# A fused attention and gated feed-forward block: who gets which of two accumulator banks

## The chip, the core and the metric

One NeuronCore of a Trainium2 chip runs the whole kernel. The time is that of one execution on the device, in microseconds (us), and the number compared is the median over several executions. The engines in the profile: PE is TensorE (PEld its weight loads), DVE VectorE, ACT ScalarE, POOL GpSimd, and SP issues most DMAs. TensorE writes only into PSUM, eight banks of 512 fp32 columns by 128 partitions; ACT and DVE read it out.

## The reference

`x` has 2048 tokens of width 512; 32 heads of width 16 attend to a window of 256 tokens; the feed-forward part has 1792 hidden columns.

```python
x = A_x
xn = _layernorm(x, axis=-1)
s = _A_ref(xn, A_wqkv, A_wo)               # causal window attention, W = 256, then @ wo
g = _silu(_B_ref(xn, B_w1, B_w3, B_w2))    # (silu(xn @ w1) * (xn @ w3)) @ w2
return x + s * g
```

## The kernel before

The tokens are cut into four tiles `t` of 512, the heads into four groups `g` of eight, the hidden columns into 14 blocks `f` of 128. Every fp32 operand is split into a high and a low f16 half, and a product is three f16 products (high by high, low by high, high by low) added up in one bank. A dense product of one 128 x 512 result is thus twelve matmuls of 512 columns, issued as two pieces of six: queries and keys (`project`, L442), values (`value`, L412), gate and up (`gate_up`, L712), down (`down`, L757), output (`total`, L799).

PSUM has three pools. `pss` (two tiles of two banks) holds the scores, `pso` (two banks) the attention's result. `psm` has the two banks that matter here; all dense products use them, and so do three short users: the transposes of an input block (`turn`, L374), the little column sums behind a weight's scale (`powers`, L222), and the transpose of the scores' maxima (`finish` in `pass1`, L511). Before, all of these ask for a tile of one tag with two buffers (`tag="mm"`), and the tile layer assigns the buffer.

Who reads a bank: a gate product is read by ACT (tanh, L723) and one step later by DVE (L727); an up product by DVE (L732); a projection by ACT (L451) and then DVE (L455); a value product by ACT (L415); a down product by DVE (L773), or ACT (L770) the first time; a turned block by ACT (L377) and then DVE (L382); maxima by ACT (L514); column sums by DVE (L224).

TensorE's order is the order in which the program issues (`ORDERED`); the other engines' order is set by a scheduler with priorities (`urgent` raises one). The attention goes by 32 units (a tile, a group, half of its heads). In each unit `batches` makes small batches of score matmuls, `pass1` for the unit after next (scores, row maxima on DVE, L500) and `pass2` for this one (scores again, L547; mask, L554; exponentials, L557; times values, L573), and `spread` lays the pieces of dense products between them. After each batch and each piece with matmuls, `step` counts `now` up by one and runs what `later(n, f)` put off by `n` steps.

In the first tile (t = 0) the feed-forward weights arrive as fp32 (`load`, L647 and L649), are squared and summed for a scale (`measure`, `squares`, L197 and L199), and split (`split_pool`: ACT scales in place, L246, ACT makes the high half, L247, POOL the low one, L243). The halves go to DRAM (L717, L760) and are loaded from there for the other tiles. All of these tiles live in 32 slots of SBUF of one size: `take` takes the slot that has been free longest, `give` puts one back, and the tile layer makes the new owner wait for the last reader of the old one. SP issues the DMAs in order, so a load that waits for its slot holds back those behind it.

```python
    def take(dtype):
        slot = free.pop(0)
...
    def give(*tiles):
        for made in tiles:
            free.append(held.pop(id(made))[0])
```

Of the kernel before, what the change touches and what calls it, by code (L numbers as in the profile page):

```python
# [76 lines left out]
def tile_block(ctx: ExitStack, tc: tile.TileContext, x, wqkv, wo, w1, w3, w2, out):  # L77
# [18 lines left out]
    psm = pool("psm", 2, PSUM)  # L96
# [4 lines left out]
    free = [f"slot{i}" for i in range(SLOTS)]  # L101
    held = {}

    def take(dtype):
# [5 lines left out]
    def give(*tiles):  # L110
        for made in tiles:
            free.append(held.pop(id(made))[0])
# [11 lines left out]
    now = [0]  # L124
# [20 lines left out]

    def flush():
        while queue:
            step()

# [30 lines left out]

    V = const.tile([P, VB, H * VW + DH], F32, name="V")
# [7 lines left out]
    def squares(parts, on_act=0, apart=0):  # L189


        ssq = small.tile([P, len(parts)], F32, name="ssq")

        def one(i, raw):
            sq = ppool.tile([P, D], BF16, name="sqa" if i < on_act else "sqd", bufs=2)
# [12 lines left out]
        def cast():  # L208
            nc.vector.tensor_copy(sb, ssq)
        if apart:  # L210
            later(apart * (len(parts) + 1) // 2, cast)
        else:
            cast()
        return sb

    def powers(sb, n, p2, inv):


        ps = psm.tile([P, n], F32, name="ps", tag="mm") if started else pss.tile([P, 2, 512], F32, name="s")[:, 0, 0:n]
        m = sb.shape[-1] // n  # L220
        for i in range(m):
            nc.tensor.matmul(ps, onesb, sb[:, i * n:(i + 1) * n], start=i == 0, stop=i == m - 1)  # L222
        al = small.tile([P, n], F32, name="al")
        nc.vector.tensor_scalar(al, ps, 2.08, 1e-30, op0=ALU.mult, op1=ALU.max)  # L224
# [103 lines left out]
    def prepare(t):  # L328
# [32 lines left out]
        def turn(b):  # L361
            if t not in X:
                X[t] = xpool.tile([P, NC, TW], F16, name="XH"), xpool.tile([P, NC, TW], F16, name="XL")
            xh, xl = X[t]
            c = slice(b * P, (b + 1) * P)

            if t or b == 3:
                pt = psm.tile([P, NC, P], F32, name="mm", tag="mm")
            elif b == 2:
                pt = pso.tile([P, 2, TW], F32, name="po")[:, 0, :].rearrange("p (k q) -> p k q", q=P)  # L370
            else:
                pt = pss.tile([P, 2, 512], F32, name="s")[:, 0, :].rearrange("p (k q) -> p k q", q=P)
            for k in range(NC):
                nc.tensor.transpose(pt[:, k, :], xts[b][:, k * P:(k + 1) * P], identf)  # L374
            give(xts.pop(b))
            with urgent():
                lasts["xh"] = nc.scalar.copy(xh[:, :, c], pt)  # L377

            def rest():
                turned[t] = turned.get(t, 0) + 1  # L380
                with urgent():
                    lasts["x"] = nc.vector.tensor_sub(xl[:, :, c], pt, xh[:, :, c])  # L382
            later(1, rest)
        return load, stats, rstd, centre, turn

    def prepare_beside(t):
# [9 lines left out]
        return made, [(0, lambda b=b: later(1 + 2 * b, lambda: turn(b))) for b in range(4)]  # L396

    def value(j):
# [4 lines left out]
        def part(half):  # L403
# [3 lines left out]
            if half == 0:  # L407
                cell["pv"] = psm.tile([P, D], F32, name="mm", tag="mm")
# [17 lines left out]
    def project(t, g, k, terms=(range(3),)):  # L426
# [7 lines left out]
        def part(n):  # L434
# [3 lines left out]
            if n == 0:  # L438
                cell["pp"] = psm.tile([P, TW], F32, name="mm", tag="mm")
# [13 lines left out]
            def rest():  # L453
# [9 lines left out]
                give(both)  # L463
# [16 lines left out]
    def pass1(t, g, p):  # L480
# [3 lines left out]
        nm = small.tile([P, 2, 16], F16, name="nm")  # L484
# [23 lines left out]
        def finish():  # L508
            qa = QA[t, g]
            pm = psm.tile([32, P], F16, name="pm", tag="mm")  # L510
            nc.tensor.transpose(pm, nm.rearrange("p b i -> p (b i)"), identh)  # L511
            mt = small.tile([32, P], F16, name="mt")
            with urgent():
                nc.scalar.copy(mt, pm)  # L514
# [138 lines left out]
    def measure(f, apart=0):  # L653
# [4 lines left out]
        def scale():  # L658
# [10 lines left out]
            def cut(i):  # L669
                a = [take(F16) for _ in range(2)]  # L670
                WF[0, f + i] = [a, None]
                for k in range(2):
                    split_pool(a[k][:, 0:D], a[k][:, D:], raws[i][k], pi[:, k, i:i + 1])
                give(*raws[i])
            later(1, lambda: cut(0))
            later(2, lambda: cut(1))
        later(5 if apart else 4, scale)

    def measure_down(k):
# [10 lines left out]
        def cut(f):  # L690
            raw2 = RAW.pop(f)[1]
            WF[0, f][1] = b = take(F16)
            split_pool(b[:, 0:D], b[:, D:], raw2, sw[:, f - f0:f - f0 + 1])
            give(raw2)
# [6 lines left out]
    def gate_up(t, f):  # L701
        cell = {}

        def part(k, half):
# [3 lines left out]
            if half == 0:  # L708
                cell[k] = psm.tile([P, TW], F32, name="mm", tag="mm")
# [8 lines left out]
            give(w)  # L718
# [10 lines left out]
            else:  # L729
# [5 lines left out]
                def rest():  # L735
                    nc.scalar.copy(hh[:, 0:TW], sg)  # L736
                    halves(nc.gpsimd.tensor_sub, hh[:, TW:], sg, hh[:, 0:TW])
                    give(sg)
# [6 lines left out]
    def down(t, k, b):  # L745
# [4 lines left out]
        def part(fs):  # L750
            if fs[0] == f0:
                cell["ps"] = psm.tile([P, D], F32, name="mm", tag="mm")
# [27 lines left out]
    def total(t, b):  # L780
# [4 lines left out]
        def part(half):  # L785
            WOH, WOL = SQ["wo"][:2]
            tb = slice(b * P, (b + 1) * P)
            if half == 0:
                cell["ps"] = psm.tile([P, D], F32, name="mm", tag="mm")
# [11 lines left out]
            if half:  # L801
# [7 lines left out]
                give(y, XR[t, b])  # L809
        return opening([(6, lambda h=h: part(h)) for h in range(2)])  # L810

    def total_by_columns(t, b):
# [9 lines left out]
        for c in (slice(0, 256), slice(256, 512)):  # L822
            ps = psm.tile([P, 256], F32, name="mm", tag="mm")
# [70 lines left out]
    def batches(u, ahead):  # L894
# [10 lines left out]
        for k, pair in enumerate(pairs):  # L905
            take_cols = not ahead or (k and k % 2 == 0 if u else k == 1)

            def batch(pair=pair, end=k == len(pairs) - 1, take_cols=take_cols):
# [7 lines left out]
                if end and cols1:  # L916
                    late.append(cols1)
                for c in ready:
                    c()
            made.append((COLS * 2 * take_cols if u else 0, batch))  # L920
        return made

    def spread(made, dense):
# [4 lines left out]
        for k, (cost, batch) in enumerate(made):  # L928
# [3 lines left out]
            while dense and (at + dense[0][0] / 2 <= whole * (k + 1) / len(made) or dense[0][0] == 0):  # L932
                c, piece = dense.pop(0)
                at += c
                piece()
                if c:
# [3 lines left out]
    def run(dense):  # L940
        for c, piece in dense:
            piece()
            if c:
# [32 lines left out]
    def keep_busy(n):  # L976
        ps = psm.tile([P, 4, P], F32, name="ps", tag="mm")
# [28 lines left out]
    k00, q00 = (project(0, 0, k, ((0,), (1,), (2,))) for k in (1, 0))  # L1006
# [19 lines left out]
    run(project(0, 1, 0))  # L1026
    later(1, lambda: fetch(0, 1))
    measure(2, 1)
    run(value(0))
# [8 lines left out]
    later(3, qk[3][2])  # L1038
    later(5, qk[3][3])
# [23 lines left out]
    for n, u in enumerate(units):  # L1063
# [7 lines left out]
        if n == 7:  # L1071
            wout[1](2)
            later(12, wout[2])
            later(14, lambda: wout[3](2))
            later(15, out_scale)
# [9 lines left out]
    while late:  # L1085
# [4 lines left out]
        step()  # L1090
    for b in range(2):
# [33 lines left out]
```

## Time and profile before

| | |
|---|---|
| median of 3 runs | 892.08 us (892.05 to 895.04) |
| the profiled execution | 886.62 us |
| its span, first to last instruction | 884.4 us |
| mean granted clock of TensorE | 0.992 |
| moved by DMA | 110.56 MB |

A row of a group gives line, engine, operation, names, shapes and count, then busy time and mean duration of one (ns), then the engine's idle time before these instructions and what ended it. A row of the order of time gives start, duration, engine, line and names, and in brackets the idle time before with its releaser. Matmuls overlap, so their mean duration is longer than the time from one to the next.

### The profile page before, as it was taken

How to read it: one execution, taken by the hardware profiler on the slowest of the kernel's cores; microseconds unless marked ns; L12 is line 12 of the kernel's file. 1: busy time of each engine (PE TensorE's matmuls, PEld its weight loads, DVE VectorE, ACT ScalarE, POOL GpSimd, SP SyncE). 2: the span in 40 equal slices, each digit the busy share in tenths (PEclk: the TensorE clock that was granted, in tenths of full speed). 3: DMA queues.
4: the chain of work that ended last, by engine and by line, in shares of the span. 5: the costliest groups of instructions: out<-in, count | busy, mean ns of one | idle time of the engine just before them, and what ended most of it. 6: DMA issues, size and time to landing. Idle time of an engine off the chain costs nothing.

```text
span 884.4 us, 21601 instructions
## 1 busy us (share of the span) xinstructions
PE 839.2 (95%) x8327; PEld 370.2 (42%) x8327; DVE 602.3 (68%) x1961; ACT 415.4 (47%) x618; POOL 196.4 (22%) x314
## 2 busy tenths in 40 slices
PE   7898868999999999999999999999999999999997
PEld 3344324444444444444444444444444444444443
DVE  7787665777667657786767766676666777666335
ACT  6886666473434444334344344443444434443521
POOL 2255254242111202111120112120211103131211
PEclk9999999999999999999999999999999999999999
DMA  9974444636633434444334433534452353332301
GB/s 290 240 257 148 151 130 120 197 92 208 157 107 90 113 103 120 126 136 106 108 114 114 115 99 84 157 113 101 119 134 70 100 153 104 100 109 69 80 9 60
DMA packets 95318, 110.56 MB, mean 125 GB/s; under 512 B 17200, under 2 KB 60528, under 8 KB 95216
## 3 DMA queue, kind: packets, MB, share of 16 engines
q1 hardware_dynamic: 94928, 108.67, 43.5%
q8 instruction: 65, 1.06, 0.5%
q10 hardware_dynamic: 288, 0.52, 0.2%
q14 instruction: 37, 0.30, 0.1%
HBM read 76.28 MB, written 28.57 MB: 119 GB/s over the span
## 4 chain that ended last, share of the span: by engine, by line
PE 66%; DVE 12%; ACT 7%; issue 6%; POOL 4%; DMA 4%; SPq 1%; POOLq 0%; ACTq 0%; DVEq 0%
PE mm L712 24%; PE mm L757 14%; PE po L573 7%; PE mm L442 6%; PE s L547 4%; POOL slot L243 4%; PE s L495 4%; PE mm L799 3%; PE mm L412 3%; DVE junk L500 3%; ACT pt L557 2%; DVE s L554 2%; DMA slot<-in_B_w_dram 1%; DVE slot L732 1%; DMA dr<-dd 1%
## 5 line engine op out<-in xcount | busy, mean ns | idle before, releaser
L712 PE MATMUL mm<-XH,slot 128*128 128x512 f16 x896 | 269.7, 383 | 8.6 <-DVE slot L455 4.0
L243 POOL TENSOR_TENSOR slot<-slot,slot 128x256 f16<-128x256 f32 (+1 forms) x220 | 147.4, 696 | 499.9 <-ACT slot L736 350.3
L557 ACT ACTIVATE pt<-s,es 128x1024 f32<-128x1024 f32 x152 | 168.9, 1114 | 181.3 <-DVE s L554 175.9
L500 DVE CUSTOM_DVE_ANT_0 junk<-s,MW 128x320 bf16<-128x320 f32 x448 | 217.8, 486 | 43.6 <-PE s L495 33.7
L712 PEld LDWEIGHTS <-slot 128*128 128x128 f16 x1344 | 123.4, 98 | 167.0 <-issue 29.0
L554 DVE TENSOR_TENSOR s<-s,MK 128x256 f32<-128x256 f32 (+2 forms) x280 | 121.1, 435 | 76.7 <-PE s L547 70.8
L712 PE MATMUL mm<-XL,slot 128*128 128x512 f16 x448 | 170.8, 381 | 0.0
L757 PE MATMUL mm<-slot,slot 128*128 128x512 f16 x672 | 157.6, 382 | 0.6 <-DVE XL L382 0.2
L757 PEld LDWEIGHTS <-slot 128*128 128x128 f16 x672 | 61.9, 98 | 80.8 <-issue 12.1
L573 PE MATMUL po<-pt,V 64*32 64x320 f32 (+4 forms) x2880 | 89.7, 347 | 0.0
L495 PE MATMUL s<-KA,qa 48*64 48x320 f16 (+2 forms) x1024 | 72.8, 299 | 12.2 <-DVE M L500 6.2
L547 PE MATMUL s<-qa,KA 50*64 50x320 f16 (+3 forms) x1472 | 62.5, 261 | 4.3 <-DVE M L500 3.3
L736 ACT CAST slot<-slot 128x512 f16<-128x512 f32 x56 | 34.5, 616 | 62.0 <-DVE slot L732 61.6
L723 ACT ACTIVATE slot<-mm,sgs 128x512 f32<-128x512 f32 x56 | 38.4, 685 | 47.1 <-PE mm L712 44.3
L547 PEld LDWEIGHTS <-KA 50*64 50x64 f16 x1472 | 31.4, 105 | 68.4 <-issue 34.4
L243 POOL TENSOR_TENSOR on<-on,rb 128x256 f32<-128x256 f32 x32 | 23.1, 744 | 163.0 <-DMA qa<-dm 98.3
L727 DVE SCALAR_TENSOR_TENSOR slot<-slot,mm 128x512 f32<-128x512 f32 x56 | 38.4, 686 | 28.9 <-ACT slot L723 28.9
L732 DVE SCALAR_TENSOR_TENSOR slot<-mm,slot 128x512 f32<-128x512 f32 x56 | 38.5, 688 | 25.9 <-PE mm L712 25.3
L573 PEld LDWEIGHTS po<-pt,V 64*32 64x32 f32 x2880 | 43.8, 106 | 28.0 <-issue 7.2
L773 DVE SCALAR_TENSOR_TENSOR slot<-mm,dsc,slot 128x512 f32<-128x512 f32 x48 | 35.9, 748 | 26.3 <-PE mm L757 26.1
L442 PE MATMUL mm<-XH,whi 128*128 128x512 f16 x128 | 47.3, 381 | 4.7 <-DVE slot L455 1.6
L495 PEld LDWEIGHTS <-qa 48*64 48x64 f16 x1024 | 29.9, 106 | 45.2 <-issue 23.9
(129 smaller groups left out, 829.8 us busy)
## 6 DMA issues: line engine op xcount, KB each, us to landing
slot<-dW SPq DMA_DIRECT2D x126, 256.0 KB
slot<-in_B_w_dram SPq DMA_DIRECT2D x42, 256.0 KB
dW<-slot SPq DMA_DIRECT2D x42, 256.0 KB
slot<-in_A_x_dram SPq DMA_DIRECT2D x30, 256.0 KB
KA<-dK SPq DMA_DIRECT2D x24, 288.0 KB
qa<-dQ SPq DMA_DIRECT2D x32, 192.0 KB
dK<-slot SPq DMA_DIRECT2D x16, 256.0 KB
dQ<-slot SPq DMA_DIRECT2D x16, 256.0 KB
```

Source lines behind the costliest of these rows:

```text
L243: op(out[:, c], a[:, c], b[:, c])
L442: nc.tensor.matmul(cell["pp"], a[:, k, c, :], b[:, c, :], start=(c, i) == parts[0][0], stop=(c, i) == parts[-1][-1])
L495: nc.tensor.matmul(s[64 * c:64 * c + 64, r, :n], qa[rows, 2 * p + a, ii * P + 64 * c:ii * P + 64 * c + 64], ka[rows, 2 * p + a, e - n:e], ...
L500: nc.vector.tensor_tensor_reduce(out=junk[:, :n], in0=s[:, r, :n], in1=mask, scale=1.0, scalar=NEG, op0=ALU.add, op1=ALU.max, accum_out=M[ ...
L547: nc.tensor.matmul(s[64 * h:64 * h + 64, r, o:o + 64 * n], ka[rows, 2 * p + a, 64 * (m + 4):64 * (m + 5)], qa[rows, 2 * p + a, 64 * (m + k ...
L554: nc.vector.tensor_add(v, v, MK[:, kind, of:of + n, :].unsqueeze(1).to_broadcast([P, 2 * len(which), n, 64]))
L557: nc.scalar.activation(pt, s, AF.Exp, scale=es)
L573: nc.tensor.matmul(cell["po"][32 * i:32 * i + 32, h, 64 * (m + k):64 * (m + k + n)], V[64 * h:64 * h + 64, (4 * t + m // 2) % VB, hd * VW: ...
L712: nc.tensor.matmul(cell[k], w[:, (a * NC + c) * P:(a * NC + c + 1) * P], b[:, c, :], start=c == 0 and i == 0, stop=c == NC - 1 and i == 2)
L723: nc.scalar.activation(sg, cell[0], AF.Tanh, scale=sg_scale[:, f:f + 1])
L732: nc.vector.scalar_tensor_tensor(sg, cell[1], 0.5 * HS / (WS * XS)**2, sg, op0=ALU.mult, op1=ALU.mult)
L757: nc.tensor.matmul(ps, hh[:, a * TW + b * P:a * TW + (b + 1) * P], w[:, c * D:(c + 1) * D], start=f == f0 and i == 0, stop=f == f1 - 1 and ...
```

## The change

- `psm` gets one buffer for each of two tags, m0 and m1. `bank` gives a dense product the bank that the last dense product didn't have; a short user takes that other bank too, without moving the turn on.
- `later_in_bank` and `pump` put work off that uses a bank for a short time: it runs at the first piece, not before its due step, that leaves a product open. The scales of weights, the maxima's transposes and the turning of blocks go there. The maxima are transposed three steps after the last batch that made them; before, two batches into the next unit.
- The maxima stand in 32 columns of a 128 x 128 tile of zeros (three such tiles), and the whole tile is transposed.
- In the start-up, projections of group 0 (keys), group 1 (queries) and the first value product use score banks, and the turned blocks change places (two in `psm`, one each in `pso` and `pss`).
- `give` may say that a tile will still be read for some steps; `take` takes the slot whose reading ends first by that count.
- The four splits of a pair of blocks come one by one, 1, 2, 4 and 6 steps after their scale.

```diff
-    psm = pool("psm", 2, PSUM)
+    psm = pool("psm", 1, PSUM)
...
     def take(dtype):
-        slot = free.pop(0)
+        free.sort()
+        slot = free.pop(0)[2]
...
+    def give(*tiles, after=0):
         for made in tiles:
-            free.append(held.pop(id(made))[0])
+            given[0] += 1
+            free.append((now[0] + after, given[0], held.pop(id(made))[0]))
...
+    def later_in_bank(n, f):
+        made_so_far[0] += 1
+        banked.append((now[0] + n, made_so_far[0], f))
+
+    def pump():
+        due = min((q for q in banked if q[0] <= now[0]), default=None)
+        if due is not None:
+            banked.remove(due)
+            due[2]()
...
+    def bank(shape, dtype=F32, short=False):
+        b = 1 - open_bank[0]
+        if not short:
+            open_bank[0] = b
+        return psm.tile(shape, dtype, name=f"m{b}", tag=f"m{b}", bufs=1)
...
+    NM = [const.tile([P, P], F16, name=f"NM{i}") for i in range(3)]
+    for nm in NM:
+        nc.gpsimd.memset(nm, 0.0)
...
-            if t or b == 3:
-                pt = psm.tile([P, NC, P], F32, name="mm", tag="mm")
+            if t:
+                pt = bank([P, NC, P], short=True)
+            elif b < 2:
+                pt = bank([P, NC, P])
...
-        return made, [(0, lambda b=b: later(1 + 2 * b, lambda: turn(b))) for b in range(4)]
+        return made, [(0, lambda b=b: later_in_bank(1 + 2 * b, lambda: turn(b))) for b in range(4)]
...
-                cell["pp"] = psm.tile([P, TW], F32, name="mm", tag="mm")
+                cell["pp"] = pss.tile([P, 2, TW], F32, name="s")[:, 0, :] if scores_bank else bank([P, TW])
...
-        nm = small.tile([P, 2, 16], F16, name="nm")
+        whole = NM[(2 * (t * NG + g) + p) % len(NM)]
+        nm = whole[:, 0:32].rearrange("p (b i) -> p b i", b=2)
...
-            pm = psm.tile([32, P], F16, name="pm", tag="mm")
-            nc.tensor.transpose(pm, nm.rearrange("p b i -> p (b i)"), identh)
+            pm = bank([P, P], F16, short=True)
+            nc.tensor.transpose(pm, whole, identh)
...
-                nc.scalar.copy(mt, pm)
+                nc.scalar.copy(mt, pm[0:32])
...
-            later(1, lambda: cut(0))
-            later(2, lambda: cut(1))
-        later(5 if apart else 4, scale)
+            for i in range(2):
+                for k in range(2):
+                    later((1, 2, 4, 6)[2 * i + k], lambda i=i, k=k: cut(i, k))
+        (later_in_bank if started else later)(5 if started else 9 if apart else 6, scale)
...
-            give(w)
+            give(w, after=4 * (t == 0))
...
-                if end and cols1:
-                    late.append(cols1)
                 for c in ready:
                     c()
+                if end and cols1:
+                    later_in_bank(3, cols1)
...
     def run(dense):
         for c, piece in dense:
             piece()
+            if started and is_open([(c, piece)]):
+                pump()
             if c:
                 step()
```

More of the change, by code (lines that the diff above doesn't have):

```diff
@@ L123, in tile_block @@
     queue = []
-    now = [0]
+    banked = []
     started = []
@@ L216, in powers @@
     def powers(sb, n, p2, inv):
-        ps = psm.tile([P, n], F32, name="ps", tag="mm") if started else pss.tile([P, 2, 512], F32, name="s")[:, 0, 0:n]
+        ps = bank([P, n], short=True) if started else pss.tile([P, 2, 512], F32, name="s")[:, 0, 0:n]
         m = sb.shape[-1] // n
@@ L407, in part @@
             if half == 0:
-                cell["pv"] = psm.tile([P, D], F32, name="mm", tag="mm")
+                cell["pv"] = pss.tile([P, 2, D], F32, name="s")[:, 0, :] if scores_bank else bank([P, D])
             pv = cell["pv"]
@@ L976, in keep_busy @@
     def keep_busy(n):
-        ps = psm.tile([P, 4, P], F32, name="ps", tag="mm")
+        ps = bank([P, 4, P], short=True)
         for _ in range(n):
@@ L1090, in tile_block @@
         step()
+    while banked:
+        step()
+        pump()
     for b in range(2):
```

59 lines of the change are left out of this document (31 added, 28 removed).

## The prediction

> **What bounds the kernel now.** I read the page's busy shares first, then busy time by stretches, then TensorE's waits, then the order of time around the longest of them.
>
> ```profile
> span 884.4 us, 21601 instructions
> ...
> PE 839.2 (95%) x8327; PEld 370.2 (42%) x8327; DVE 602.3 (68%) x1961; ACT 415.4 (47%) x618; POOL 196.4 (22%) x314
> ```
>
> TensorE (PE) is busy 95% of the span and no other engine over 68%, so the kernel ends when TensorE has issued its work, and the change adds or removes no product. What can be won is TensorE's idle time and time in which it runs below its pace. The stretches (columns: length, then busy time of PE, PEld, DVE, ACT, POOL, granted clock, DMA share, GB/s) say where that is:
>
> ```profile
> 0.00:40.00 40.00, 31.81 (x158) 14.54 (x159) 30.48 (x113) 28.02 (x59) 7.61 (x34) 1.00 0.97 267
> ...
> 80.00:120.00 40.00, 35.13 (x326) 15.15 (x325) 27.95 (x115) 25.20 (x46) 10.60 (x16) 0.96 0.43 135
> 120.00:160.00 40.00, 29.79 (x246) 13.17 (x244) 22.83 (x82) 27.10 (x48) 22.61 (x34) 0.88 0.49 153
> ...
> 600.00:700.00 100.00, 99.46 (x1084) 43.22 (x1083) 68.06 (x218) 40.33 (x52) 15.28 (x24) 1.00 0.42 112
> ```
>
> In 0 to 40 us TensorE is idle for 8.2 us, in 80 to 120 for 4.9, in 120 to 160 for 10.2; in 600 to 700 for 0.5. After about 165 us, once the weights are split, there is hardly anything to win. What TensorE waited for (total us, times, longest us):
>
> ```profile
> PE s L495 <- DVE M L500: 6.2, 7, 1.4
> PE s L495 <- ACT pt L557: 4.6, 12, 0.9
> PE mm L712 <- DVE slot L455: 4.0, 2, 3.1
> ...
> PE mm L712 <- DVE slot L727: 2.3, 3, 1.1
> PE mm L374 <- DVE slot L727: 2.3, 1, 2.3
> PE mm L412 <- DVE slot L455: 1.7, 1, 1.7
> PE mm L442 <- DVE slot L455: 1.6, 1, 1.6
> ...
> PE mm L374 <- DVE al L224: 1.3, 1, 1.3
> PE mm L712 <- DVE slot L732: 1.2, 1, 1.2
> PE mm L374 <- DVE slot L455: 1.2, 2, 1.0
> PE mm L442 <- DVE al L224: 1.1, 2, 0.9
> ...
> PE mm L712 <- ACT mt L514: 0.5, 1, 0.5
> ```
>
> Two kinds. The first two rows are score tiles (banks of the pool `pss`, which the change leaves alone). The next nine are a first matmul that waits until the last reader of one of the two `psm` banks is done: 4.0 + 2.3 + 2.3 + 1.7 + 1.6 + 1.3 + 1.2 + 1.2 + 1.1 = 16.7 us. That is what choosing banks can reach, 1.9% of the span.
>
> **The change part by part.** *Start-up (projections and values on score banks).* Two of the nine rows lie here:
>
> ```profile
> 22.50 1.02 PE L442 MATMUL mm<-XH,whi 128*128 128x512 f16 x4 [1.62 <-DVE slot L455]
> ...
> 24.50 0.16 DVE L224 TENSOR_SCALAR al<-s 128x1 f32<-128x1 f32 x1 [0.24 <-PE s L222]
> ...
> 25.46 2.56 ACT L237 ACTIVATE wvh<-slot,swwv 128x512 f16<-128x512 f32 x4 [3.89 <-DVE swwv L233]
> ```
>
> The 1.62 us at 22.50 delay the little matmul behind the scale of wv, DVE waits for that, and ACT stands 3.89 us for DVE: this wait is on the chain, and a third bank removes it: -1.6. The 1.7 us of L412 come while ACT works through its squares, which decide when TensorE goes on at 37 us; I count 0 for them, cover being ACT's work; without it they are worth 1.7. Bounds 0 and -3.3.
>
> *Dense banks alternated by hand, short users on the other bank.* I set the matmul order of both kernels side by side and counted the 512-column matmuls between the last matmul on a `psm` bank and the next tenant's first. Before, 35 openings have fewer than six in between, 76 have six to eleven, 184 more. Now 10, 124 and 159. No dense product follows a dense product on its bank after fewer than nine any more (15 did after fewer than six), 54 instead of 27 of the 61 short users stand inside a product, and every short user has at least six behind the product whose bank it takes. What six matmuls cover: matmuls of 512 columns follow each other at 0.22 us (18 in 3.99 us, the stretch of L757 quoted further down), so six are 1.3 us. A gate product has two readers, one after the other, all others one or two of like length:
>
> ```profile
> L723 ACT ACTIVATE slot<-mm,sgs 128x512 f32<-128x512 f32 x56 | 38.4, 685 | 47.1 <-PE mm L712 44.3
> ...
> L727 DVE SCALAR_TENSOR_TENSOR slot<-slot,mm 128x512 f32<-128x512 f32 x56 | 38.4, 686 | 28.9 <-ACT slot L723 28.9
> ```
>
> 685 + 686 ns = 1.37 us if both start at once. So nine matmuls cover a prompt eviction of any kind, six almost. With the waits of the trace laid onto those counts, openings under six matmuls waited 10.8 us; 1.6 of that is the start-up wait above, 1.9 waits for new data or the warm-up matmuls, not a bank. The other 7.3 us are each at most 1.3 us long, and six more matmuls cover 1.3: -7 (bounds -7.3, and -3 if evictions get later). Against that, seven dense products open three to five matmuls behind a short user; a prompt pair of readers of 1.3 us is then short by 0.2 to 0.6 us: +1.5 (0 to +3). And six to eleven is more frequent. Up to 165 us it occurred 16 times with 4.9 us of waits, 0.31 us each; now it occurs 30 times there, +4.3 if the mean holds, 0 if evictions are prompt; since nearly half of the 4.9 us is one event that the next part treats, +2. After 165 us it costs 0.01 us each (0.6 us in 60), so nothing.
>
> *Splits one by one, slots by age.* The longest waits have this behind them (order of time of SP's queue, POOL, ACT and DVE):
>
> ```profile
> 113.50 0.95 SPq L647 DMA_DIRECT2D slot<-in_B_w_dram  x2
> ...
> 122.01 11.89 POOL L243 TENSOR_TENSOR slot<-slot,slot 128x256 f16<-128x256 f32 x18 [8.53 <-PE mm L442]
> ...
> 127.56 0.60 ACT L451 ACTIVATE slot<-mm 128x512 f16<-128x512 f32 x1 [0.64 <-POOL slot L243]
> ...
> 128.19 0.69 DVE L455 SCALAR_TENSOR_TENSOR slot<-mm,slot 128x512 f16<-128x512 f32 x1 [2.44 <-ACT slot L451]
> ...
> 131.33 0.69 ACT L723 ACTIVATE slot<-mm,sgs 128x512 f32<-128x512 f32 x1 [0.64 <-POOL slot L243]
> ...
> 132.05 0.69 DVE L727 SCALAR_TENSOR_TENSOR slot<-slot,mm 128x512 f32<-128x512 f32 x1 [1.97 <-ACT slot L723]
> ```
>
> The last weight loads of a group went out at 113.50, having waited for slots; nine splits then came at once, POOL worked 11.89 us without a pause, ACT's copies took slots that POOL was still reading, and the evictions L451 and L723 queued behind them on ACT. TensorE waited 3.1 us (L712 on L455) and 2.3 us (L374 on L727). In the change the four splits of a pair are issued one, two, four and six steps after their scale instead of two at one and two at two, and slots are handed out by the step of their last use, not by when they were given back. I counted the age of the slot that each load takes: the six loads of this group took slots given back 13, 10, 7, 6, 4 and 1 steps earlier, now 13, 13, 17, 10, 7 and 6, so the last two loads can leave some five steps sooner. But 32 slots stay 32 slots, at one point one is free in both, and ACT's splits take slots of an age of two or less no less often. Half of the event, then.
>
> Behind such waits TensorE also runs slower:
>
> ```profile
> 106.00:110.00 4.00, 3.69 (x10) 1.34 (x10) 3.67 (x15) 1.38 (x3) 0.00 (x0) 0.57 0.02 4
> ...
> 130.00:134.00 4.00, 1.69 (x10) 0.88 (x12) 0.77 (x2) 1.87 (x4) 3.85 (x7) 0.52 0.68 243
> 134.00:137.00 3.00, 3.00 (x20) 1.20 (x17) 1.43 (x5) 1.64 (x2) 0.00 (x0) 0.50 0.47 137
> ...
> 157.00:160.00 3.00, 3.00 (x10) 1.04 (x8) 1.27 (x6) 2.76 (x7) 0.00 (x0) 0.58 0.81 278
> ```
>
> At a granted clock c, a busy time b holds b(1 - c) of delay: 1.69 x 0.48 + 3.00 x 0.50 = 2.3 us at 130 to 137, 3.69 x 0.43 = 1.6 at 106, 3.00 x 0.42 = 1.3 at 157. The event with its clock is 3.1 + 2.3 + 2.3 = 7.7 us; half is -3.8 (0 to -7.7). Of the other two, 2.9 us, I take a quarter, -0.7 (-2.9, and +2 if a new cluster of waits brings another). The Trainium skill (TensorE: Matmul & The Clock Gate, section "HAM oscillation") puts the fall of the clock down to an idle window of about 3.4 us; by that, taking away waits of 1 to 2 us returns no clock, and the sum would be 1.8 us smaller. The rows don't agree: the longest wait of all is 3.1 us, and the clock fell at 106 behind a wait of 0.5 us (L712 on L514).
>
> *Maxima transposed at 128 columns, inside a product.*
>
> ```profile
> 306.46 0.31 PE L495 MATMUL s<-KA,qa 48*64 48x320 f16 x4
> 306.70 4.06 PE L757 MATMUL mm<-slot,slot 128*128 128x512 f16 x18
> 310.69 0.42 PE L547 MATMUL s<-qa,KA 50*64 50x320 f16 x12
> 310.94 0.31 PE L495 MATMUL s<-KA,qa 48*64 48x320 f16 x4
> 311.18 0.23 PE L511 MATMUL pm<-identh,nm 128*32 128x128 f16 x1
> 311.33 1.09 PE L573 MATMUL po<-pt,V 64*32 64x320 f32 x32
> ```
>
> From scores to the next work takes 0.24 us (306.46 to 306.70) with no transpose, and with one 0.24 + 0.15. So each of the 32 costs 0.15 us. Among full-array matmuls it can cost as little as its 128 columns, a quarter of 0.22 = 0.055 us, or as much as its own duration of 0.23. It is nearest to a stream of full-array matmuls, whose weight load hides only partly behind 128 columns, so I take 0.10: 32 x -0.05 = -1.6 (-3.1 to +2.6). The Trainium skill (same page, "Part 4: PE-mode transpose") gives about 275 ns for a 128x128 transpose in a kernel; by that this part would be +4.0. No row here shows one so long.
>
> Three memsets on POOL at the start and one buffer fewer for squares cost nothing: POOL is busy 7.6 of the first 40 us, and the buffer's writers all sit on DVE, in order. The DMAs of the maxima leave SP's queue earlier than before, a unit ahead of their use.
>
> Sum: -1.6 - 7 + 1.5 + 2 - 3.8 - 0.7 - 1.6 = -11.2 us against the profiled execution's 886.62 us (span 884.4 and 2.2 around it), 875.4. The median of the runs, 892.08, is 1.0062 times the profiled one: 881.
>
> **The rivals.** *Waits stay where evictions are late.* Up to 165 us the evictions are late, not the banks short: openings of twelve and more matmuls waited there too, 4.7 us in 26. With the means of the trace before (0.74, 0.31 and 0.18 us up to 165 us; 0.11, 0.01 and 0 after) on the new counts (4, 30, 20; 6, 94, 139) the waits are 17.4 us against 21.1: -3.7 and nothing else, 888.3. For it speaks the stretch at 122; against it that no dense product follows another closely.
>
> *Weights come late (slower).* The last split of a pair is issued four steps later, a step being six matmuls, 1.3 us, or with a batch of scores about 1.9. The products that use it start that much later if its lead is smaller. One row is near it:
>
> ```profile
> L712 PEld LDWEIGHTS <-slot 128*128 128x128 f16 x1344 | 123.4, 98 | 167.0 <-issue 29.0 <-POOL slot L243 4.5 <-DMA slot<-dW 0.2
> ```
>
> The weight loads of L712 did wait 4.5 us for POOL's splits, hidden so far behind the products in front. If three pairs lose 4 x 1.3 = 5.2 us each, that is +15.6, and with the other terms +4.4 on the profile: 896.5; with steps of 1.9 it is 904. It decides from a lead of under four steps. Against it: most leads in the trace are over 13 us.
>
> *The transposes cost what the page says.* -11.2 + 1.6 + 4.0 = -5.6: 886.4, still a gain.
>
> **How the numbers follow.** Half a per cent, 4.5 us, is what a measurement of this kernel tells from no change. The forecast 881 has 0.58, the rival of late evictions 0.20, late weights 0.18, dear transposes 0.04. The first alone spans 873 (the event and the clock gone whole) to 887 (the event kept, half-covers dear). The range 873 to 896 leaves out the worse half of the late weights and a little below. Faster: 0.58 and the transposes' 0.04, less a little of both at the edge, 0.60; same 0.22; slower 0.18.
>
> **What would show it.** Right: the rows of L712, L442 and L412 waiting on L455, L727 and L732 fall to under 5 us in all; TensorE's idle time in 120 to 160 us halves and its clock there is over 0.94; the transposes stand between L712 or L757 rows and the next matmul follows in about 0.1 us. Wrong: waits of L511, L374 or L222 on L727, L732 or L773 (short users inside a product, waiting for the bank), or L712's matmuls waiting for POOL's L243.

## The result, and the profile after

The changed kernel takes 888.21 us (median of 20 runs, 883.78 to 892.49), the kernel before, run beside it, 892.09 (20 runs, 889.17 to 900.53). The ratio is 0.9946 with a 95% interval of 0.9923 to 0.9968: faster, by 3.9 us at the medians, a third of the forecast 11.2.

The two profiled executions don't show it at their ends: 886.62 us before, 887.07 after. The profiled execution of before is faster than any of the 20 runs beside it, so what follows compares stretches and waits of profiles, and takes the size of an effect from the medians.

The page after:

```profile
span 885.3 us, 21595 instructions
...
PE 837.1 (95%) x8327; PEld 368.2 (42%) x8327; DVE 602.3 (68%) x1961; ACT 411.9 (47%) x618; POOL 196.0 (22%) x317
```

Nothing has changed in what bounds the kernel. I cut both profiles where ACT copies out the eighth unit's result (`os`, at 275.0 us before and 273.7 after). Up to there the weights are split, behind it they come ready from DRAM. Busy time by stretch, before:

```profile
0.00:275.00 275.00, 244.28 (x2120) 109.52 (x2121) 194.82 (x726) 167.61 (x298) 89.75 (x156) 0.98 0.60 174
275.00:884.40 609.40, 594.94 (x6209) 260.71 (x6207) 407.50 (x1236) 247.82 (x322) 106.62 (x158) 1.00 0.37 103
```

and after:

```profile
0.00:274.00 274.00, 245.53 (x2126) 109.02 (x2127) 196.74 (x729) 167.49 (x298) 91.16 (x161) 0.98 0.60 174
274.00:885.30 611.30, 591.60 (x6203) 259.16 (x6201) 405.55 (x1233) 244.39 (x321) 104.80 (x157) 1.00 0.37 103
```

The second stretch takes 2 us longer, though TensorE is busy some 3 us less: it is idle 5.2 us more, 0.4 of them behind its last matmul. That isn't the scatter of one execution: from the eighth `os` to the end it takes 609.4, 610.3 and 610.6 us in the profiles that have the old banks (before, e1 and e9 below) and 611.6, 611.6, 611.6 and 611.9 in four with the new ones (after, e4, e5, e7). So the gain at the medians must lie ahead of it. What TensorE waits for there, before:

```profile
PE s L495 <- ACT pt L557: 3.8, 10, 0.9
PE s L547 <- DVE M L500: 2.1, 3, 0.9
PE s L495 <- DVE M L500: 1.4, 2, 0.9
PE s L547 <- ACT pt L557: 1.0, 2, 0.6
PE mm L799 <- ACT O L623: 0.8, 1, 0.8
PE mm L712 <- DVE slot L727: 0.4, 1, 0.4
```

and after (L529 is L495 of before, L581 L547, L545 the transpose L511, L792 the down product L757, L415 and L548 the readers L382 and L514):

```profile
PE s L529 <- ACT pt L591: 4.7, 11, 0.9
PE s L581 <- DVE M L534: 3.0, 6, 0.9
PE m L545 <- DVE NM L540: 1.8, 1, 1.8
PE m L792 <- DVE XL L415: 1.8, 2, 1.6
PE m L792 <- ACT mt L548: 1.6, 2, 0.9
PE s L529 <- DVE M L534: 1.4, 2, 1.1
```

Three rows are new, and all three belong to short users: a transpose that comes before its maxima are there, and dense products that open behind a short user's last reader. Adding up each first matmul's wait by the kind of tile that it writes, dense banks and everything that isn't a score tile made TensorE wait 2.3 us behind the eighth unit before and 6.1 after, score tiles 8.5 and 9.4: 4.7 us are lost.

Up to the eighth unit the same sums are 21.1 and 15.2 us for the banks, 9.6 and 13.3 for score tiles. These two must not be set off against each other, since in the first 40 us projections that wrote a `psm` bank now write a score tile. The longest rows of the changed kernel up to there:

```profile
PE s L529 <- DVE M L534: 6.0, 5, 2.5
PE s L253 <- DVE sb L240: 3.5, 2, 3.3
PE m L792 <- DVE slot L762: 3.1, 1, 3.1
PE m L545 <- DVE slot L762: 2.9, 2, 1.8
PE m L792 <- DVE XL L415: 2.2, 2, 1.8
```

The second row is a column sum of the start-up that waits for its squares, which is a wait for data. In the first 40 us the banks went from 6.5 to 1.6 us and the score tiles from 1.7 to 4.5; from there to the eighth unit the banks went from 14.6 to 13.5 only, the score tiles from 8.0 to 8.8. This pair is a poor witness for that stretch, though: there the two profiles of e1 and e9, with the old banks, have bank waits of 18.4 and 19.3 us, and nine of experiments with the new banks (e2 to e8, e10 and e11) 10.5 to 14.9. With those of before and after, the mean is 17.4 for the old banks and 12.5 for the new, and that of the score waits 9.4 and 10.4.

### The profile page after: what moved, and what is told of

The parts are those of the page before. It is cut to its first block, busy times and chain, and to the rows that moved or that the text cites. A ratio compares the mean times of both kernels' runs of the same rounds, so it can differ in the third digit from the quotient of the medians.

```text
span 885.3 us, 21595 instructions
## 1 busy us (share of the span) xinstructions
PE 837.1 (95%) x8327; PEld 368.2 (42%) x8327; DVE 602.3 (68%) x1961; ACT 411.9 (47%) x618; POOL 196.0 (22%) x317
## 4 chain that ended last, share of the span: by engine, by line
PE 63%; DVE 12%; DMA 8%; ACT 6%; issue 5%; POOL 3%; SPq 2%; POOLq 0%; ACTq 0%; DVEq 0%
PE m L747 23%; PE m L792 12%; PE po L607 7%; PE m L475 6%; PE s L529 4%; PE s L581 4%; PE m L834 4%; PE m L445 4%; ACT pt L591 3%; DVE junk L534 3%; POOL slot L274 3%; DMA slot<-in_B_w_dram 2%; DVE s L588 2%; DMA slot<-in_A_x_dram 1%; DMA dK<-slot 1%
## 5 line engine op out<-in xcount | busy, mean ns | idle before, releaser
L747 PE MATMUL m<-XH,slot 128*128 128x512 f16 x896 | 268.8, 382 | 1.9 <-DVE slot L762 1.1
L747 PEld LDWEIGHTS <-slot 128*128 128x128 f16 x1344 | 122.1, 98 | 158.4 <-issue 23.7
L747 PE MATMUL m<-XL,slot 128*128 128x512 f16 x448 | 170.6, 381 | 0.0
L792 PE MATMUL m<-slot,slot 128*128 128x512 f16 x672 | 159.6, 382 | 9.0 <-DVE XL L415 4.0
L792 PEld LDWEIGHTS <-slot 128*128 128x128 f16 x672 | 61.1, 98 | 89.0 <-issue 18.3
L529 PE MATMUL s<-KA,qa 48*64 48x320 f16 (+2 forms) x1024 | 73.0, 299 | 13.3 <-DVE M L534 7.4
L581 PE MATMUL s<-qa,KA 50*64 50x320 f16 (+3 forms) x1472 | 62.3, 261 | 5.0 <-DVE M L534 3.0
L771 ACT CAST slot<-slot 128x512 f16<-128x512 f32 x56 | 34.5, 616 | 65.1 <-DVE slot L767 64.6
L581 PEld LDWEIGHTS <-KA 50*64 50x64 f16 x1472 | 31.3, 105 | 70.2 <-issue 37.4
L758 ACT ACTIVATE slot<-m,sgs 128x512 f32<-128x512 f32 x56 | 38.3, 684 | 43.0 <-PE m L747 42.5
L767 DVE SCALAR_TENSOR_TENSOR slot<-m,slot 128x512 f32<-128x512 f32 x56 | 38.6, 689 | 25.6 <-PE m L747 24.9
L762 DVE SCALAR_TENSOR_TENSOR slot<-slot,m 128x512 f32<-128x512 f32 x56 | 38.3, 684 | 24.2 <-ACT slot L758 24.0
L808 DVE SCALAR_TENSOR_TENSOR slot<-m,dsc,slot 128x512 f32<-128x512 f32 x48 | 35.9, 748 | 23.9 <-PE m L792 23.7
L529 PEld LDWEIGHTS <-qa 48*64 48x64 f16 x1024 | 29.6, 106 | 45.3 <-issue 25.0
L475 PE MATMUL m<-XH,whi 128*128 128x512 f16 x120 | 45.1, 384 | 0.4 <-ACT mt L548 0.4
```

The source lines that it names most:

```text
L475: nc.tensor.matmul(cell["pp"], a[:, k, c, :], b[:, c, :], start=(c, i) == parts[0][0], stop=(c, i) == parts[-1][-1])
L529: nc.tensor.matmul(s[64 * c:64 * c + 64, r, :n], qa[rows, 2 * p + a, ii * P + 64 * c:ii * P + 64 * c + 64], ka[rows, 2 * p + a, e - n:e], ...
L581: nc.tensor.matmul(s[64 * h:64 * h + 64, r, o:o + 64 * n], ka[rows, 2 * p + a, 64 * (m + 4):64 * (m + 5)], qa[rows, 2 * p + a, 64 * (m + k ...
L747: nc.tensor.matmul(cell[k], w[:, (a * NC + c) * P:(a * NC + c + 1) * P], b[:, c, :], start=c == 0 and i == 0, stop=c == NC - 1 and i == 2)
L758: nc.scalar.activation(sg, cell[0], AF.Tanh, scale=sg_scale[:, f:f + 1])
L767: nc.vector.scalar_tensor_tensor(sg, cell[1], 0.5 * HS / (WS * XS)**2, sg, op0=ALU.mult, op1=ALU.mult)
```

## Experiments

Each ran beside the kernel before on the same chip; the ratios are to that.

**Width without the new place.** The kernel before with the wide tile:

```diff
-            pm = psm.tile([32, P], F16, name="pm", tag="mm")
-            nc.tensor.transpose(pm, nm.rearrange("p b i -> p (b i)"), identh)
+            pm = psm.tile([P, P], F16, name="pm", tag="mm")
+            nc.tensor.transpose(pm, whole, identh)
```

> The kernel before with one part of the change: the maxima stand in a 128 x 128 tile of zeros and the whole tile is transposed, at the old place between two batches of the attention. Theory A (the 3 us that the transposes save come from their new place among full-array matmuls, not from the width): the transpose here still stands between two array shapes, from its start to the next matmul 0.15 to 0.2 us instead of 0.15, time within 2 us of before. Rival B (the width alone saves it): the next matmul follows in about 0.06 us and the kernel is 3 us faster than before, 0.997.

0.9987 (0.9964 to 1.0011), 891.19 us: no change, theory A. TensorE's order of time around one of them (L515 is L511 there):

```profile
410.51 0.31 PE L499 MATMUL s<-KA,qa 48*64 48x320 f16 x4
410.75 0.23 PE L515 MATMUL pm<-identh,NM 128*128 128x128 f16 x1
410.91 0.77 PE L577 MATMUL po<-pt,V 64*32 64x320 f32 x16
```

The next matmul follows after 0.16 us, as with the narrow transpose. The width alone saves nothing between two other array shapes (48*64 ahead of it, 64*32 behind it).

**The new place without the width.** The changed kernel with `whole[:, 0:32]` transposed:

> The changed kernel with the maxima transposed at 32 columns again, at their new place inside a dense product. Theory A (a change of array shape costs about 0.1 us on either side): 0.2 to 0.3 us from the transpose's neighbours instead of 0.06, 32 x 0.2 = 6 us slower than the changed kernel, so 2 us slower than before, 1.002. Rival B (the shape of one transpose inside a product costs nothing): as the changed kernel, 0.995.

0.9989 (0.9967 to 1.0012), 891.5 us: 3.3 us above the changed kernel at the medians. Around a transpose, here and then in the changed kernel:

```profile
403.87 0.38 PE L475 MATMUL m<-XL,whi 128*128 128x512 f16 x1
404.18 0.23 PE L545 MATMUL m<-identh,NM 128*32 128x128 f16 x1
404.34 0.39 PE L475 MATMUL m<-XH,whi 128*128 128x512 f16 x1
```

```profile
402.39 0.38 PE L475 MATMUL m<-XL,whi 128*128 128x512 f16 x1
402.60 0.22 PE L545 MATMUL m<-identh,NM 128*128 128x128 f16 x1
402.66 0.38 PE L475 MATMUL m<-XH,whi 128*128 128x512 f16 x1
```

Narrow, it takes 0.31 + 0.16 us from one matmul of the product to the next; wide, 0.21 + 0.06, and 0.22 is the plain distance. The 0.2 us between the two comes with the other array shape, on the way into it and out of it, so theory A has the mechanism; 32 x 0.2 = 6.4 us, of which the medians show half. The stretch behind the eighth unit is 5.5 us longer than in the changed kernel: 23 transposes stand in it, 4.6 us, and the profile has 3.4 us at a clock of 0.50 at 553.8, up to 1.7. Width and place pay only together, and 0.06 is at the lower of the two bounds of the prediction.

**Short users a little off.** The changed kernel with two delays altered:

```diff
-                    later_in_bank(3, cols1)
+                    later_in_bank(4, cols1)
...
-            later(1, rest)      # low half of a turned block
+            rest()
```

> The changed kernel with two delays of short users altered: the maxima are transposed four steps after their last batch instead of three, and the low half of a turned block is read out in the same step as the high half, not one step later. Theory A (after 165 us the change's gain is given back by dense products that wait for a short user's readers, and by transposes that wait for the maxima): the waits of L757's product on the turned block's low half, 4.0 us in the changed kernel, and of the transposes on the maxima, 2.4 us, fall to 2 us together; 4 us faster than the changed kernel, 0.990 of before. Rival B (those waits only stand in for others): they fall, score waits rise by as much, 0.995.

0.9921 (0.9891 to 0.9951), 885.74 us: 2.5 us faster than the changed kernel at the medians, though the two intervals overlap. The transposes' waits for their maxima fall from 2.4 us to 0.6; the products' waits for the turned block's low half fall only from 4.0 to 3.3 (the 1.57 us at 479 stays to the hundredth). The waits for score tiles don't rise, so rival B has nothing for it. The first half of theory A holds, the second hardly. Why not stands in DVE's order of time in the changed kernel, while a block is turned inside a down product:

```profile
476.86 0.08 DVE L534 DVE_READ_ACCUMULATOR2_ANT M<- 128x1 f32 x1
477.50 0.75 DVE L808 SCALAR_TENSOR_TENSOR slot<-m,dsc,slot 128x512 f32<-128x512 f32 x1 [0.56 <-PE m L792]
478.29 0.69 DVE L415 TENSOR_TENSOR XL<-m,XH 128x512 f16<-128x512 f32 x1
```

DVE stands idle for 0.56 us at L808, the eviction of the very product that is still open, and L415, which empties the short user's bank, is queued behind it. TensorE's next product (L792 at 479.03) then waits for both.

**Turned blocks only where six matmuls follow.** The same, and no turned block in a down product with three matmuls left:

```diff
+        if f1 - f0 < 4:
+            made[0][1].tight = True
...
-        due = min((q for q in banked if q[0] <= now[0]), default=None)
+        due = min((q for q in banked if q[0] <= now[0] and not (tight and q[3])), default=None)
```

> The kernel e3_short_users, and turned blocks are no longer put into products that have only three matmuls left. Theory A (a turned block's second reader on DVE stands behind the eviction of the very product that it was put into, so the next dense product waits for both; with six matmuls behind it the wait is 1 us shorter): the waits of L757's products on the turned block's low half fall from 3.1 to under 1.5 us; 1.5 us faster than e3_short_users, 0.990 of before. Rival B (DVE is late anyway): the waits move to the next product, 0.992.

0.9919 (0.9901 to 0.9938), 885.39 us, against 0.9921: the time is the same within what the runs can tell. In the profile the waits of L792 on the turned blocks fall to 1.4 us in all, and those on the maxima's copy rise from 1.6 to 2.5 us behind the eighth unit, since maxima now take the places with three matmuls. Theory A's wait went, rival B has the time. This is the fastest version of the study, below the kernel before by the whole interval; its interval and the changed kernel's overlap.

**Splits in pairs again; slots first in, first out again; the start-up as before.** Three undone parts of the changed kernel:

```diff
-                    later((1, 2, 4, 6)[2 * i + k], lambda i=i, k=k: cut(i, k))
+                    later(1 + i, lambda i=i, k=k: cut(i, k))
```

> The changed kernel with the four splits of a pair issued as before, two one step and two two steps after their scale. Theory A (before 165 us the evictions are late for other reasons, so spacing the splits moved waits but took none away): bank waits up to 165 us as in the changed kernel, 11 to 13 us, time within 2 us of it, 0.993 to 0.997 of before. Rival B (the spacing is what relieved the pile of splits that held TensorE for 5.4 us at 126 to 133 us before): that pile is back, 4 us slower than the changed kernel, 0.999.

0.9988 (0.9972 to 1.0003), 891.06 us: by its time rival B, and without the spacing a wait of 3.5 us is back at 132 to 136 us. But the bank waits as a whole are no longer than in the changed kernel, 12.9 us up to the eighth unit against 15.2, with 16.2 against 13.3 at score tiles. What is longer is the time at half clock (see the last section): seven lengths of it in the profile against four, up to 5.1 us, and over all executions a mean clock of 0.990 against 0.992, up to 1.9 of the 2.9 us. So it isn't shown that the wait for the pile makes the difference.

```diff
-        free.sort()
```

> The changed kernel with the slots handed out in the order in which they were given back, as before. Theory A (32 slots are nearly all in use where it matters, so the order hardly changes who waits): as the changed kernel, 0.993 to 0.997 of before. Rival B (slots by age brought the loads forward): ACT waits more for POOL's reading of slots and the last loads of a group leave some us later; 3 us slower, 0.998.

1.0015 (1.0002 to 1.0028), 893.95 us: rival B again, and twice its size. At the medians the sort is worth 5.7 us in the changed kernel; the eighth unit ends at 279.9 us instead of 273.7.

> The changed kernel with the start-up as before: turned blocks, projections and the first value product on their old kinds of bank. Theory A (the start-up gain is real: in the changed kernel the column sum behind L222 ran at 34.2 us against 35.9 before): it runs at about 35.9 again, 1.8 us slower than the changed kernel, 0.9965 of before. Rival B (what the start-up wins is lost again by 80 us to loads that land when they land): as the changed kernel, 0.9946.

0.9943 (0.9923 to 0.9964), 887.44 us: rival B. The column sum runs at 36.1 us, in the changed kernel at 34.2, so the start-up does win 1.9 us. ACT copies out the first unit's result (`os`) at 95.65 and 94.88 us, the second's at 121.79 and 121.81: 0.8 us is left of it after one unit, nothing after two.

**Slots and splits without the banks; banks without slots, splits and width.**

> The kernel before with two parts of the change alone: slots by age and the splits one by one. Banks, maxima and start-up as before. Theory A, after the runs that undid single parts (slots by age worth 5.7 us, splits 2.9, the wide transposes 3.3, the start-up nothing, 3.9 in all): if the parts add up, these two alone are worth about 8 us, 0.991 of before, and more than the whole change. Rival B (they help only beside the banks, since the short users they protect are placed anew): within 2 us of before, 0.998 to 1.002.

1.003 (1.0008 to 1.0052), 894.14 us: slower than before, where the undone parts had promised 8 us. The profile, of the slowest of its 12 executions, has a wait of 4.6 us at 83 to 87 us and one of 3.1 at 136 to 139 for L727's product that way too.

> The changed kernel with slots in the order given back, splits in pairs and the maxima transposed at 32 columns: what stays is the banks by hand, the short users inside products and the start-up. Theory A (the parts add up, so the banks cost what the others bring beyond 3.9 us): 6 to 8 us slower than before, 1.008. Rival B (the banks by themselves are neutral, the other parts overlap): 4 us slower than before at most, which the narrow transposes inside products explain alone, 1.000 to 1.004.

1.0057 (1.0038 to 1.0077), 896.81 us, 4.9 us slower than before: between the two theories. By the rows of e2 a narrow transpose costs 0.31 + 0.16 - 0.22 = 0.25 us inside a product, against 0.16 at its old place, so the narrow transposes make some 3 us of these. Neither of the two sets of parts is a gain alone; the parts don't add up.

**What the early waits hang on.** First the loads of the second token tile, a unit earlier:

> The changed kernel with the four loads of the second token tile moved to the unit before, nothing else. Theory A (the longest waits for a bank before 165 us come from DVE and ACT standing in order behind statistics and squares whose loads landed late): DVE's wait of 4.3 us for the load of x at 80 to 85 us goes, and TensorE's 3.1 us wait for L727's product behind it; up to 3 us faster than the changed kernel, unless the weight loads, now later in SP's order, hold up the squares on ACT by as much. Rival B (the bank's own turn is what makes that wait): TensorE's wait of 3.1 us stays.

0.9972 (0.9949 to 0.9995), 890.35 us, 2.1 us above the changed kernel. The wait of 3.1 us at 85 us is gone, and a wait of 3.9 us of a transpose for L727's product stands at 74 to 78: neither theory, the wait has moved. Then, on the fastest version, the statistics of that tile behind the gate product in DVE's order (the edit also issues the statistics of the third and fourth tile one step later):

```diff
+            with (tc.issue_after(lasts["evict"].ins) if t == 1 else nullcontext()):
                 nc.vector.bn_stats(st, xts[b])
```

> The kernel e8_turns_six with the statistics of the second token tile one step later and, in DVE's order, behind the last gate product issued before them. Theory A (TensorE's longest wait, 2.8 us at 83 to 86 us, is for L727's product on DVE that stands behind statistics whose load has not landed, though the product's tanh had been done for 4 us): that wait goes; up to 3 us faster than e8_turns_six, 0.989 of before. Rival B (DVE is free earlier, but the next weights land no sooner, and TensorE waits for them): the wait goes and another of like size comes up to 165 us, 0.992.

0.9983 (0.9963 to 1.0003), 890.82 us, 5.4 us slower than without it. What this was aimed at, in DVE's order of time in the changed kernel:

```profile
80.34 0.08 DVE L534 DVE_READ_ACCUMULATOR2_ANT M<- 128x1 f32 x1
84.67 0.69 DVE L371 BATCH_NORM_STATS2 st<-slot 128x6 f32<-128x512 f32 x1 [4.25 <-DMA slot<-in_A_x_dram]
85.40 0.18 DVE L372 BATCH_NORM_AGGREGATE mv<-st 128x2 f32<-128x6 f32 x1
86.48 0.69 DVE L371 BATCH_NORM_STATS2 st<-slot 128x6 f32<-128x512 f32 x1 [0.90 <-DMA slot<-in_A_x_dram]
87.09 0.67 DVE L762 SCALAR_TENSOR_TENSOR slot<-slot,m 128x512 f32<-128x512 f32 x1
```

DVE waits 4.25 us for a load, and L762 (L727 of before) empties a bank only at 87.09. In the experiment L727's product runs at 79.36 and that wait is gone. In its place, up to 275 us (lines are one further on in this run):

```profile
PE s L530 <- DVE M L535: 7.9, 4, 3.5
PE m L748 <- DVE slot L763: 4.7, 1, 4.7
PE s L530 <- ACT pt L592: 4.0, 2, 3.6
```

The kernel that it was made from, e8, had 7.9, 1.1 and 0.9 us in these rows. From 40 us to the eighth unit the banks wait 10.5 us (11.0 in e8), score tiles 14.7 (9.4): rival B in kind, and worse than its time. Of the 5.4 us up to 2.1 go with the clock, at a mean of 0.989 against 0.991.

**Maxima out of the dense banks.** The last experiment asks the same of the stretch behind the eighth unit:

```diff
-            pm = bank([P, P], F16, short=True)
+            pm = pss.tile([P, 2, 512], F32, name="s")[:, 0, 0:P // 2].bitcast(F16)
```

> The changed kernel with the maxima transposed into a score tile (one of the two of the pool pss) instead of a dense bank; place and width stay. From the end of the eighth unit (about 274 us) to the end TensorE waited 2.3 us for dense banks and 8.5 us for score tiles in the kernel before, 6.1 and 9.4 in the changed kernel, and that stretch took 609.4 and 611.6 us. Theory A (the later 3.8 us of bank waits are those of and behind the maxima): bank waits fall to about 3 us there; if score tiles have room, the stretch takes 3 us less than in the changed kernel, 608.5 us, and the kernel is at 0.991 of before. Rival B (a wait saved on a dense bank is paid at the scores, since ACT and DVE read both in their own order): bank waits fall, score waits rise by as much or more, the stretch takes 611 us or more, 0.995.

1.0096 (1.0064 to 1.0129), 900.54 us. Bank waits fall from 6.1 to 3.1 us, as theory A has it, score waits rise from 9.4 to 23.4, and the stretch takes 625.3 us:

```profile
PE s L545 <- DVE M L534: 12.5, 18, 1.0
PE s L529 <- ACT pt L591: 4.3, 10, 0.9
PE s L545 <- ACT pt L591: 2.3, 2, 1.2
PE s L545 <- DVE NM L540: 1.8, 1, 1.8
```

Eighteen times a transpose waits for a score tile whose maxima DVE is still taking. That is rival B's sign and more than its time, but not its reason: the three rows of L545, 16.6 us, are the transposes themselves, 14.8 of it as new tenants of score tiles, and the attention's own matmuls wait 6.7 us there instead of 9.4. What is shown is that these tiles take the transposes only with a wait. Up to the eighth unit the same edit doesn't hurt: the unit ends at 269.7 us instead of 273.7.

## Why the prediction was wrong

**Dense after dense: right.** The step "no dense product follows a dense product on its bank after fewer than nine" did what it says. The waits of a dense product behind a dense product (the rows of L712, L412 and L442 on L455, L727 and L732) fell from 10.8 to 4.2 us, 6.6 for the 7 that I took, though these aren't the same waits: 3.3 of the 10.8 are the two rows of the start-up. What is left, 3.1 and 1.1 us, has twelve matmuls in between and is a late eviction.

**The step that failed: "After 165 us it costs 0.01 us each (0.6 us in 60), so nothing."** Openings with six to eleven matmuls behind the last tenant waited 0.6 us in 60 before and 4.8 in 95 now, 0.05 each. I took the mean of openings of one mixture and gave it to another: in the new one dense products that open behind a short user waited 2.0 us in 32, those behind a dense product nothing in 26, and short users 2.8 in 37. Two things were not in the old mean. A short user inside a product has its second reader in DVE's queue behind the eviction of that same product (478.29 above). And a transpose three steps after its batch can be earlier than its maxima: 2.4 us of waits that the prediction counted nowhere, of which one more step removed 1.8. Beside it, the term of +1.5 for dense products three to five matmuls behind a short user was too small: 3.0 us in six openings after 165 us, its upper bound. So the stretch behind the eighth unit, for which the terms gave some -3.5 us (2.3 of bank waits, and 23 transposes at 0.05), came out 2.2 us longer: 3.8 more at the banks, 0.9 at the scores, 0.4 behind the last matmul, and 3.0 less of busy time, 2.4 of it by the transposes. That is 5.7 of the 7.3 us by which the forecast missed, an estimate, since it adds a difference of profiles to one of medians.

**The early part: near the forecast by the medians, not seen in this pair.** If the stretch behind the eighth unit loses 2.2 us and the whole gains 3.9, the part ahead of it gained some 6 of the 7.7 us that its terms gave. The pair of profiles shows 1.3, and why the profiled execution of before was so fast in it is open. The event at 122 to 137 us went almost whole: from 120 to 160 us TensorE is idle for 4.6 us instead of 10.2 and its clock is 0.96 instead of 0.88, as the signs for "right" had it. But from 80 to 120 us it is idle for 7.9 instead of 4.9, with a wait of 3.1 us behind a late load of x. The first sign for "wrong" came, too: short users inside a product (L545, L407, L253) waited 4.1 us for the readers L762 and L767. That a wait removed at a bank comes back at the score tiles is shown for a small part at best: from 40 us to the eighth unit the means given above are 4.9 us lower at the banks and 1.0 higher at the scores, and one execution differs from the next by more than that 1.0.

**The first rival had the time.** 888.3 against 888.21. Its reason, late evictions, is shown for the early stretch, where openings of twelve and more matmuls still waited 4.2 us (4.7 before); that it named 3.7 us of bank waits "and nothing else" is a coincidence of a gain at the transposes and losses at the short users.

**Start-up: the wait went, the gain didn't.** The 1.6 us became 1.9 at 34 us, as argued, and e7 shows nothing of them left by 122 us.

**Splits and slots: too small in the changed kernel, and of the wrong sign alone.** The term was -3.8 for half of one event. Undone, slots cost 5.7 us and splits 2.9, up to 1.9 of these by the clock; without the banks the two make the kernel 0.3% slower. What the order of slots does to each load's moment was followed in one group only, and why the gain needs the banks is open.

**Transposes: the right mechanism, mis-sized.** I took 0.10 us each instead of 0.15. It was 0.16 (0.159 in most) and is 0.06, the lower bound: 23 x 0.10 = 2.4 us behind the eighth unit alone, instead of 1.6 in all. Nothing here shows the 275 ns that the Trainium skill (TensorE: Matmul & The Clock Gate, "Part 4: PE-mode transpose") gives for a kernel's context; the rival built on it falls.

**Late weights: didn't happen.** No row of the changed kernel has TensorE's matmuls waiting for POOL's splits, and its weight loads of gate and up products waited 1.9 us for them, 4.5 before.

**The clock: of the order of the quarter that I took off.** The two profiles have the same time at half clock. Over executions the mean granted clock is 0.992 in the 20 of the changed kernel and 0.990 in the 92 of the kernel before that ran beside the experiments: at 885 us that is 1.5 us at most, for the -0.7 of the forecast. Whether fewer waits caused it wasn't tested.

## What to carry to other kernels

Where one engine's waits are many and small, ask of each what the engine would wait for next if it were gone: e4 and e11 each removed the wait that they aimed at, and another of like size came up. When waits are added up by the buffer's name, look first whether the change moved work from one name to the other. Count covers for each kind of user apart, with its readers and with what stands ahead of them in their queue: a mean over openings of another kind is no price. And transpose in the shape that the array already has, among work of that shape.

## What the runs showed of the hardware that was not expected

TensorE's clock drops to half in stretches of 3.41 us, or of twice that. In the changed kernel the records of the granted clock have 0.5 in 34.5 to 37.9, 89.1 to 92.5, 119.8 to 123.2 and 174.4 to 177.8 us, each 3.41 us; the kernel before had four such lengths, too (one of 6.83 us counts twice). Around the first, at 0.50 and with TensorE busy nearly all the time (busy time by stretches):

```profile
30.00:34.40 4.40, 1.15 (x12) 0.60 (x10) 1.64 (x12) 4.40 (x15) 0.00 (x0) 1.00 1.03 268
34.50:37.80 3.30, 3.23 (x15) 1.17 (x11) 2.50 (x16) 2.96 (x5) 1.49 (x2) 0.50 1.02 201
37.90:42.00 4.10, 4.10 (x27) 1.71 (x26) 2.12 (x10) 2.86 (x6) 1.56 (x3) 1.00 0.52 120
```

Each length costs up to 1.7 us, and how many an execution gets varies: one of them in the profile of e1, seven in that of e5. The 20 executions of the changed kernel go with it: 883.78 and 885.52 us at mean clocks of 0.996 and 0.998, 892.37 and 892.49 at 0.988. That is most of the scatter of this kernel, and more than the change is worth. With the waits it also accounts for the stretch up to the eighth unit: that unit ends between 269.7 and 286.7 us in the 14 profiles here, and with TensorE's waits and half of the time at clock 0.50 taken off, 237.4 to 241.0 us are left in each. Where two versions differ by a few us, a wait should be called the cause only after both sums have been compared.
